# VectorE sums issued behind a pair's eviction, and one more Strassen round in each of the last two chunks

## The chip, the cores and the metric

The kernel runs on one core of one Trainium2 chip. The metric is the device time of one execution in microseconds. "PE" is TensorE, "DVE" VectorE, "ACT" ScalarE, "POOL" GpSimd, "SP" SyncE; "PEld" is TensorE's loading of stationary operands, which runs beside its matmuls.

## The reference

Causal attention with 16 beacon rows ahead of the keys, followed by two matrix products with a leaky ReLU between them:

```python
# B, H, S, Nb, D = 8, 8, 576, 16, 64
k_all = np.concatenate([beacon_k, k], axis=2); v_all = np.concatenate([beacon_v, v], axis=2)
scores = scale * np.matmul(q, k_all.transpose(0, 1, 3, 2))      # causal on the 576 keys
a = softmax(scores)
attn = np.matmul(a, v_all)
x = attn.transpose(0, 2, 1, 3).reshape(B * S, H * D)            # 4608 x 512
h = x @ w_in                                                    # 512 -> 2048
out = np.maximum(0.01 * h, h) @ w_out                           # 2048 -> 512
```

Inputs and output are float32; the kernel computes its products in bfloat16 and sums in float32.

## The kernel before

**Attention.** The 64 heads are taken as 32 pairs. For a pair TensorE writes scores into PSUM (`score` for the first 8 pairs, `stretch` after them, three tiles of 512 columns in a `block`), ScalarE takes their exponentials into a buffer `aT`, GpSimd blanks the triangles above the diagonal (`triangle`, L285), and TensorE multiplies by the values (`value_matmuls`, L355) in two halves of three and two row blocks. `value` then evicts each half on VectorE: a reciprocal of the sums (L384) and a product into `x_nat` (L385). A DMA transpose turns `x_nat` into `xT`. The values of a batch come in five loads that GpSimd issues (L210), and so do queries and keys (L167).

**The two layers.** The 4608 tokens are 9 chunks of 512. `up` computes one block of 128 of the 2048 hidden columns (`moe1`, L438: four matmuls of 512 columns, then an eviction on ScalarE, L446), 16 of them a chunk. `down` computes one of 14 pieces of layer two, which is a Strassen-Winograd scheme of seven products (`moe2`, L514: eight matmuls of 256 columns a piece). That scheme needs sums of the hidden values, the token sums: `token_sums` gives four VectorE operations for each half of the columns, at L789. They wait in a list `due`, and `add_due` issues one ahead of each `up` or `down`; `add_all` issues what a chunk still lacks ahead of its third product.

**The last two chunks** (numbers 7 and 8) come after the attention. There a part of layer one is done in rounds: `in_round` computes four blocks with seven products of four 256-column matmuls each (L667) where four `up`s take sixteen of 512 columns. Its products are combined by five VectorE sums (L710, L721, L722, L724, L725) and leave over ScalarE (`leave`, L684). `last_chunks` reads the order from a string: `R111` is a round with one `down` at each of three places in it, `u` an `up`, `d` a `down`, `t` the token sums of the first half, `x` the sums of the chunk's tokens that the rounds read. Chunk 7 has two rounds and eight `up`s before the change, chunk 8 three and four.

**What sets the order.** Each engine runs its instructions in the order in which they are written. Attention and layers are interleaved by a list of events with places along the pairs. Between two events `fill` issues `up`s and `down`s, and ahead of a `value` event it does so until two (or four, where no `down` can run) stand between the last block of scores and the values. All of them, the score tiles of a block's first tile and the halves of the values share one pool of four PSUM banks (`ps_one`), handed out again in the order in which the program gives them back.

Of the kernel before, what the change touches and what calls it, by code (L numbers as in the profile page):

```python
# [15 lines left out]
def kernel(  # L16
# [11 lines left out]
    nc = tc.nc  # L28

    B, H, S, D = q.shape  # L30
# [7 lines left out]
    NF = DF // 128  # L38
    NCH = NTOK // 512
# [408 lines left out]
    HF, HD, HT = NF // 2, DM // 2, 256  # L448
# [54 lines left out]
    def ND(i):  # L503
        return 2 * len(PRODUCTS)
# [118 lines left out]
    def w_in_sums(n, lo=0, hi=ROUNDS, first=False):  # L623
        cols = slice(lo * 256, hi * 256)
        (b11, b21), (b12, b22) = (
            [w_in_sb[i][:, at : at + 2, cols] for at in (0, 2)] for i in range(2)
        )
        x, y = {5: (b12, b11), 6: (b22, w_t[5][:, :, cols]), 4: (b21, w_t[6][:, :, cols]), 7: (b22, b12)}[n]
        at = 0 if first else len(due)
        due[at:at] = [  # L630
            (TAIL - 1, dict(out=w_t[n][:, j, cols], in0=x[:, j], in1=y[:, j], op=SUB)) for j in range(2)
        ]

    def x_parts(i):
        at = i * 512 % (XR * S)
# [19 lines left out]
    def in_product(i, n, r, bank, first):  # L655
        (a11, a12), (_, a22) = x_parts(i)
        x = {1: a11, 2: a12, 4: a22}.get(n)
        x = x_sums[i][n] if x is None else x
        for f in range(2):
            cols = slice(r * 256 + f, r * 256 + f + 255, 2)  # L660
            for j in range(2):
                if n in w_t:
                    w = w_t[n][:, j, cols]
                else:
                    i0, j0 = {1: (0, 0), 2: (0, 2), 3: (1, 2)}[n]
                    w = w_in_sb[i0][:, j0 + j, cols]
                nc.tensor.matmul(  # L667
                    out=bank[:, f * HT : (f + 1) * HT],
                    lhsT=w,
                    rhs=x[:, j],  # L670
                    start=first and f == 0 and j == 0,
                    stop=j == 1,
                    skip_group_check=True,
                )

    leaves = []

    def leave_all(n=3):
        while leaves and n:
# [11 lines left out]
    def in_round(i, r, downs):  # L691
        if i not in gT:
            gT[i] = gpool.tile([128, NF, 512], BF16, name="gT")
        add = nc.vector.tensor_tensor

        def bank():
            return ps_one.tile([128, 512], FP32, name="acc", tag="one")

        one = bank()
        in_product(i, 1, r, one, True)  # L700
        nc.scalar.copy(out=temps["p1"], in_=one)
        leave_all(1)
# [18 lines left out]
        add(out=temps["u3"], in0=seven, in1=temps["u2"], op=ADD)  # L721
        add(out=temps["c21"], in0=four, in1=temps["u3"], op=ADD)  # L722
        in_product(i, 3, r, five, False)
        add(out=temps["c12"], in0=five, in1=temps["u2"], op=ADD)  # L724
        add(out=temps["c22"], in0=temps["u3"], in1=temps["p5"], op=ADD)  # L725
        leaves.extend(((i, 2 * r, 1, temps["c21"]), (i, HF + 2 * r, 0, temps["c12"]), (i, HF + 2 * r, 1, temps["c22"])))
        for _ in range(downs[2]):
            down()
        done1[0] += 4

    def last_chunks(steps):
        for step in steps.split():
            op, n = step[0], int(step[1:] or 1)
            i = done1[0] // NF
            if op == "d":
                for _ in range(n):
                    down()
            elif op == "u":
                for _ in range(n):
                    leave_all()  # L740
                    up()
            elif op == "R":
                in_round(i, done1[0] % NF // 4, [int(x) for x in step[1:]])
            elif op == "X":
                x_transposes(n, nc.vector.tensor_copy)
            elif op == "w":
                w_in_sums(7, ROUNDS - 1, ROUNDS)
            elif op == "x":
                x = x_in_sums(n)
                if n == TAIL:  # L750
                    for _, op in x[:2]:
                        nc.vector.tensor_tensor(**op)
                    due[2:2] = [x[3], x[2]]
                else:
                    due.extend(x)
            elif op == "a":
                add_due(n)
            elif op == "D":
                later = due[:]
                assert len(later) == 4, len(later)  # L760
                due.clear()
                down()
                down()
                due.extend(later)
            elif op == "t":
                leave_all()
                due.extend((i, op) for op in token_sums(i, 0, SLICE))

    done1, done2, at2, ready, turn, first_down, held = [0], [0], [0, 0], [0], [0], [0], [0]

# [13 lines left out]

    due = []

    def add_due(n=1):
        while due and n:
            nc.vector.tensor_tensor(**due.pop(0)[1])  # L789
            n -= 1  # L790

    def add_all(i):
        while due and due[0][0] == i:
            add_due()

    SLICE = 4
    first_sums = {}

    def up():
        i1, n = divmod(done1[0], NF)  # L800
        assert i1 < ready[0]
        add_late()
        fc = n if i1 == 0 else n // 2 + n % 2 * HF
# [12 lines left out]
        if i1 and n % (2 * SLICE) == 2 * SLICE - 1:  # L816
            due.extend((i1, op) for op in token_sums(i1, n // 2 + 1 - SLICE, n // 2 + 1))

    def down():
        add_late()  # L820
# [130 lines left out]
    with order:  # L951
# [22 lines left out]
        def has_down():  # L974
            return at2[0] < done1[0] // NF
# [79 lines left out]
```

## Time and profile before

| | |
|---|---|
| median of three runs | 323.6 us (323.35 to 325.74) |
| the profiled execution | 323.36 us, of which the span of the trace is 321.7 us |
| TensorE busy | 315.4 us of the span (98%) |
| VectorE, ScalarE, GpSimd busy | 172.8, 207.3, 184.8 us |
| granted TensorE clock | 0.999 |

Times inside the trace are counted from the start of the span. In a timeline a row gives the start, the length from the first start to the last end, the engine, the line, the operation with its operands, and in brackets how long the engine stood idle before it and who released it. In the chain of waits a row gives start, length and what ran. In a grouped view a row ends in the busy time and the mean of one in ns.

### The profile page before, as it was taken

What the parts mean: (1) busy time and instruction counts of PE and PEld (TensorE: products, weight loads), DVE (VectorE), ACT (ScalarE), POOL (GpSimd) and SP (SyncE); (2) the same over time, 40 slices, a digit from 0 to 9 for tenths busy, and PEclk for the clock granted to TensorE, in tenths of its full rate; (3) what the DMA queues carried; (4) which work ended last, traced back from release to release, by engine and by line L of the source; (5) the groups of instructions that cost most, each with busy time, mean ns of one, the idle gap of its engine ahead of it and who ended that gap; (6) DMA issues with size and microseconds to landing.
All of it is one profiled execution on the core that took longest, in us unless ns stands there. A gap on an engine that the chain in (4) does not pass through costs nothing.

```text
span 321.7 us, 8891 instructions
## 1 busy us (share of the span) xinstructions
PE 315.4 (98%) x3578; PEld 225.0 (70%) x3578; DVE 172.8 (54%) x350; ACT 207.3 (64%) x352; POOL 184.8 (57%) x352
## 2 busy tenths in 40 slices
PE   8999999999999999999999999999999999999995
PEld 5584558765677558845888888656865687688784
DVE  3473378635365145434552454435464699577954
ACT  3979974489756786478647864787468446555510
POOL 8896939999999687659875976765221000000000
PEclk9999999999999999999999999999999999999999
DMA  7999999999999999999999999999312101200113
GB/s 133 137 199 200 137 208 134 127 189 195 139 142 177 191 136 152 122 159 117 144 154 181 111 142 117 156 159 122 71 49 87 24 0 35 92 9 7 67 61 131
DMA packets 152474, 39.51 MB, mean 123 GB/s; under 512 B 138816, under 2 KB 150208, under 8 KB 152432
## 3 DMA queue, kind: packets, MB, share of 16 engines
q0 software_dynamic: 97744, 18.54, 85.0%
q1 hardware_dynamic: 54416, 20.33, 37.4%
q8 instruction: 28, 0.46, 0.7%
q14 instruction: 14, 0.11, 0.1%
q10 hardware_dynamic: 272, 0.07, 0.1%
HBM read 37.22 MB, written 9.44 MB: 145 GB/s over the span
## 4 chain that ended last, share of the span: by engine, by line
PE 92%; ACT 5%; DVE 1%; issue 1%; ACTq 0%
PE acc L438 31%; PE acc L514 23%; PE sc L514 11%; PE av L355 9%; PE sc L310 6%; PE acc L667 5%; PE sc L263 2%; PE av L835 2%; ACT aT L329 2%; PE tp L239 2%; ACT gT L446 1%; ACT aT L325 1%; PE tp L401 1%; ACT aT L272 1%; DVE x_nat L385 0%
## 5 line engine op out<-in xcount | busy, mean ns | idle before, releaser
L438 PE MATMUL acc<-xT,w_in_sb 128*128 128x512 bf16 (+1 forms) x560 | 117.6, 355 | 0.4 <-DVE x_nat L385 0.4
L446 ACT ACTIVATE gT<-acc 128x512 bf16<-128x512 f32 x124 | 71.2, 626 | 33.0 <-PE acc L438 32.8
L285 POOL TENSOR_SCALAR_AFFINE_SELECT aT<-aT 128x256 bf16<-128x256 bf16 (+2 forms) x160 | 60.3, 406 | 53.9 <-ACT aT L325 29.6
L438 PEld LDWEIGHTS <-w_in_sb 128*128 128x128 bf16 x560 | 51.8, 98 | 43.4 <-issue 2.3
L514 PEld LDWEIGHTS <-gT 128*128 128x128 bf16 x576 | 54.9, 98 | 9.5 <-issue 2.0
L329 ACT ACTIVATE aT<-sc 128x1024 bf16<-128x1024 f32 (+3 forms) x64 | 51.8, 894 | 0.0
L514 PEld LDWEIGHTS <-gsum 128*128 128x128 bf16 x432 | 40.9, 98 | 7.6 <-issue 0.6
L325 ACT ACTIVATE aT<-sc 128x512 bf16<-128x512 f32 (+3 forms) x64 | 29.0, 521 | 23.0 <-PE sc L310 23.0
L384 DVE RECIPROCAL rec<-av 128x6 f32<-128x6 f32 (+1 forms) x64 | 11.9, 186 | 55.2 <-PE av L355 54.6
L355 PEld LDWEIGHTS <-aT 128*128 128x128 bf16 (+1 forms) x960 | 36.2, 98 | 7.6 <-issue 0.4
L355 PE MATMUL av<-v_aug,aT 128*128 128x65 bf16 (+1 forms) x960 | 38.7, 194 | 0.0
L210 POOL DMA_DIRECT2D v_aug<-in_v_dram x40 | 34.2, 864 | 3.0 <-DMA w_in_sb<-in_moe_w_in_dram 3.0
L514 PE MATMUL acc<-w_out_sb,gT 128*128 128x256 bf16 x288 | 34.6, 273 | 0.4 <-ACT gT L446 0.4
L167 POOL DMA_DIRECT2D k_nat<-in_k_dram x46 | 33.4, 733 | 0.8 <-issue 0.6
L167 POOL DMA_DIRECT2D q_nat<-in_q_dram x46 | 33.4, 731 | 0.1
L385 DVE TENSOR_TENSOR x_nat<-av,rec 128x384 bf16<-128x384 f32 (+1 forms) x64 | 31.4, 491 | 2.2
L272 ACT ACTIVATE aT<-sc 128x1024 bf16<-128x1024 f32 (+3 forms) x32 | 25.8, 872 | 3.2 <-PE sc L263 3.2
L789 DVE TENSOR_TENSOR gsum<-gT 128x1024 bf16<-128x1024 bf16 x18 | 12.4, 689 | 24.3 <-ACT gT L446 24.3
L514 PE MATMUL acc<-w_sum,gsum 128*128 128x256 bf16 x192 | 24.3, 273 | 0.0
L310 PE MATMUL sc<-qT,kT 64*128 64x80 bf16 (+22 forms) x384 | 22.2, 251 | 0.6 <-DVE x_nat L385 0.4
L310 PEld LDWEIGHTS <-kT 64*128 64x128 bf16 x384 | 12.9, 94 | 10.6 <-issue 6.7
L545 ACT COPY p<-acc 128x512 f32<-128x512 f32 x15 | 9.1, 605 | 14.9 <-PE acc L514 14.9
(95 smaller groups left out, 337.3 us busy)
## 6 DMA issues: line engine op xcount, KB each, us to landing
out_dram<-p SPq DMA_DIRECT2D x26, 256.0 KB, 2.9
q_nat<-in_q_dram POOLq DMA_DIRECT2D x46, 72.0 KB, 4.9
k_nat<-in_k_dram POOLq DMA_DIRECT2D x46, 72.0 KB, 5.3
v_aug<-in_v_dram POOLq DMA_DIRECT2D x24, 128.0 KB, 6.1
w_in_sb<-in_moe_w_in_dram POOLq DMA_DIRECT2D x2, 1024.0 KB, 11.0
w_out_sb<-in_moe_w_out_dram POOLq DMA_DIRECT2D x2, 1024.0 KB, 11.4
out_dram<-u SPq DMA_DIRECT2D x8, 256.0 KB, 3.5
gsum<-in_q_dram POOLq DMA_DIRECT2D x9, 144.0 KB, 7.5
```

The costliest lines, as they stand in the source:

```text
L167: nc.gpsimd.dma_start(out=t[:, :, par], in_=(q, k)[which][b, 2 * hp + par].rearrange("(t p) d -> p t d", p=NR),)
L210: nc.gpsimd.dma_start(out=dst[lo : ROWS[c], c, :, 0:D], in_=v[b, :, OFF[c] : OFF[c] + n].rearrange("h p d -> p h d"),)
L272: nc.scalar.activation(out=aT[:, :, c0 : c0 + w], in_=sc[:, :, 0:w], func=AF.Exp, scale=0.125)
L285: nc.gpsimd.affine_select(out=view, in_=view, compare_op=ALU.is_ge, fill=0.0, base=128 - n if lo == 0 else 0, channel_multiplier=-1, patte ...
L310: nc.tensor.matmul(out=(sc[par] if apart else sc[:, par])[:, at : at + b - a], lhsT=kT[ps_, c * 128 : (c + 1) * 128], rhs=qT[ps_, q0 : q0 ...
L325: nc.scalar.activation(out=probs[g][:, par, lo:hi], in_=sc[par][:, at : at + hi - lo], func=AF.Exp, scale=0.125)
L329: nc.scalar.activation(out=probs[g][:, :, lo:hi], in_=sc[:, :, at : at + hi - lo], func=AF.Exp, scale=0.125)
L355: nc.tensor.matmul(out=avv[:, n, 0 : D + 1], lhsT=aT[0 : ROWS[c], par, a0 : a0 + 128], rhs=va[0 : ROWS[c], c, 2 * hp + par, :], start=(c = ...
L385: nc.vector.tensor_tensor(out=x_nat[:, t0:t1].rearrange("p t e d -> p (t e) d"), in0=avv[:, :, 0:D], in1=rec[:, n0:n1, None].to_broadcast( ...
L438: nc.tensor.matmul(out=acc[:, lo:hi], lhsT=w_in_cols(fc, j), rhs=xT[:, j, x0 : x0 + hi - lo], start=(j == 0), stop=(j == NJ - 1), skip_gro ...
L446: nc.scalar.activation(out=gT[i][:, fc, :], in_=acc, func=AF.Prelu, alpha=0.01)
L514: nc.tensor.matmul(out=acc[:, lo : lo + HD], lhsT=left(i, n, fc, tile), rhs=right(n, fc), start=(lo == 0 and fc == 0), stop=(fc == HF - 1) ...
```

## The change

**Behind the eviction.** While an event `value` is prepared, `add_due` only counts what it would have issued; the operations are issued right behind that half's eviction. `add_all` now picks a chunk's operations out of the list wherever they stand, and a round first issues the sums of its chunk's tokens that are still owed.

**One more round.** Chunk 7 has three rounds and four `up`s, chunk 8 four rounds and no `up`. The weight sums of the fourth round (`w_in_last`, eight operations of 128x256) are made on GpSimd into the value buffer of the last but one batch. The sum `c22` of each round (L725 before) moves from VectorE to GpSimd. Two weight sums that were made between chunk 7 and chunk 8 are made in chunk 6.

```diff
+    flat_v = v_bufs[(B - 2) % 2].rearrange("p c h d -> p (c h d)")
+    w_last = {
+        n: flat_v[:, i * 512 : (i + 1) * 512].rearrange("p (j f) -> p j f", j=2) for i, n in enumerate((5, 6, 4, 7))
+    }
...
+    def w_in_last(n, eng):
+        cols = slice(ROUNDS * 256, (ROUNDS + 1) * 256)
...
+        for j in range(2):
+            eng.tensor_tensor(out=w_last[n][:, j], in0=x[:, j], in1=y[:, j], op=SUB)
...
     def in_product(i, n, r, bank, first):
...
+            if any(op["out"] is x for _, op in due):
+                add_all(i, [x_sums[i][m] for m in (5, 6, 3, 7)])
...
-                    w = w_t[n][:, j, cols]
+                    w = w_t[n][:, j, cols] if r < ROUNDS else w_last[n][:, j, f : f + 255 : 2]
...
-        add(out=temps["c22"], in0=temps["u3"], in1=temps["p5"], op=ADD)
+        nc.gpsimd.tensor_tensor(out=temps["c22"], in0=temps["u3"], in1=temps["p5"], op=ADD)
...
+    owed = [None]
+
     def add_due(n=1):
+        if owed[0] is not None:
+            owed[0] += n
+            return
         while due and n:
             nc.vector.tensor_tensor(**due.pop(0)[1])
             n -= 1
...
+        if (i1, n) == (TAIL - 1, 4 * ROUNDS + 1):
+            w_in_sums(7, ROUNDS - 1, ROUNDS, first=True)
+            add_due(2)
...
             elif what is value:
+                owed[0] = owed[0] or 0
                 while done1[0] + done2[0] < since + (2 if has_down() else 4) and fill(True):
                     pass
             what(*args)
+            if what is value:
+                n, owed[0] = owed[0], None
+                add_due(n)
...
-        last_chunks("D X31 x7 d a1 R111 x8 R111 t u d u d u d u u d u d u u w")
-        last_chunks("R111 R111 R111 t u d u d u d u d d d14")
+        for n in (5, 6, 4, 7):
+            w_in_last(n, nc.gpsimd)
+        last_chunks("D X31 x7 d a1 R110 R111 x8 u R311 d t u u u")
+        last_chunks("R100 R112 t d R200 R111 d d d t3 d14")
```

VectorE's order in the middle of the attention, at the first pair whose values meet the token sums of chunk 1 (`gsum` is a token sum, `gT` the hidden values and one token sum in place, `av` a half of the values in PSUM). Before:

```order
L789 TENSOR_TENSOR gsum_1608<-gT 128x1024
L789 TENSOR_TENSOR gsum_1609<-gsum_1608,gT 128x1024
L384 RECIPROCAL rec<-av 128x6
L385 TENSOR_TENSOR x_nat<-av,rec 128x384
L384 RECIPROCAL rec<-av 128x4
L385 TENSOR_TENSOR x_nat<-av,rec 128x256
L789 TENSOR_TENSOR gT<-gT 128x4x256
L789 TENSOR_TENSOR gsum_1610<-gT,gsum_1609 128x1024
```

And at the same place after the change:

```order
L384 RECIPROCAL rec<-av 128x6
L385 TENSOR_TENSOR x_nat<-av,rec 128x384
L813 TENSOR_TENSOR gsum_1608<-gT 128x1024
L813 TENSOR_TENSOR gsum_1609<-gsum_1608,gT 128x1024
L813 TENSOR_TENSOR gT<-gT 128x4x256
L813 TENSOR_TENSOR gsum_1610<-gT,gsum_1609 128x1024
L384 RECIPROCAL rec<-av 128x4
L385 TENSOR_TENSOR x_nat<-av,rec 128x256
```

The first half's eviction has moved ahead of two sums; all four sums now stand between the halves, and the second half's eviction behind four of them instead of two.

VectorE's order two pairs later, at the other half of chunk 1's token sums. Before:

```order
L789 TENSOR_TENSOR gsum_1608<-gT 128x1024
L384 RECIPROCAL rec<-av 128x6
L385 TENSOR_TENSOR x_nat<-av,rec 128x384
L384 RECIPROCAL rec<-av 128x4
L385 TENSOR_TENSOR x_nat<-av,rec 128x256
L789 TENSOR_TENSOR gsum_1609<-gsum_1608,gT 128x1024
L789 TENSOR_TENSOR gT<-gT 128x4x256
L789 TENSOR_TENSOR gsum_1610<-gT,gsum_1609 128x1024
```

And after the change:

```order
L384 RECIPROCAL rec<-av 128x6
L385 TENSOR_TENSOR x_nat<-av,rec 128x384
L813 TENSOR_TENSOR gsum_1608<-gT 128x1024
L813 TENSOR_TENSOR gsum_1609<-gsum_1608,gT 128x1024
L384 RECIPROCAL rec<-av 128x4
L385 TENSOR_TENSOR x_nat<-av,rec 128x256
L813 TENSOR_TENSOR gT<-gT 128x4x256
L813 TENSOR_TENSOR gsum_1610<-gT,gsum_1609 128x1024
```

The first half's eviction has moved ahead of one sum, and the second half's stands behind two instead of one.

GpSimd's order at the end of the program, from the triangles of the last pair on (`aT_93` is that pair's buffer, later the place of `c22`; `v_aug_88` the value buffer that takes the fourth round's weight sums). Before:

```order
L285 AFFINE_SELECT aT_93<-aT_93 128x2x112
L285 AFFINE_SELECT aT_93<-aT_93 128x2x128 x3
L285 AFFINE_SELECT aT_93<-aT_93 80x2x80
L1050 UNCONDITIONAL_BRANCH
L1050 ISA
```

And after the change:

```order
L285 AFFINE_SELECT aT_93<-aT_93 80x2x80
L645 TENSOR_TENSOR v_aug_88<-w_in_sb_83,w_in_sb_82 128x256 x2
L645 TENSOR_TENSOR v_aug_88<-w_in_sb_83,v_aug_88 128x256 x2
L645 TENSOR_TENSOR v_aug_88<-w_in_sb_82,v_aug_88 128x256 x2
L645 TENSOR_TENSOR v_aug_88<-w_in_sb_83 128x256 x2
L742 TENSOR_TENSOR aT_93<-kT 128x512 x7
```

GpSimd, which ended with the last triangles, now makes the eight weight sums behind them, and then one `c22` for each of seven rounds.

More of the change, by code (lines that the diff above doesn't have):

```diff
@@ L632, in w_in_sums @@
         ]
+    def w_in_last(n, eng):
+        cols = slice(ROUNDS * 256, (ROUNDS + 1) * 256)
+        (b11, b21), (b12, b22) = (
+            [w_in_sb[i][:, at : at + 2, cols] for at in (0, 2)] for i in range(2)
+        )
+        x, y = {5: (b12, b11), 6: (b22, w_last[5]), 4: (b21, w_last[6]), 7: (b22, b12)}[n]
+        for j in range(2):
+            eng.tensor_tensor(out=w_last[n][:, j], in0=x[:, j], in1=y[:, j], op=SUB)
     def x_parts(i):
@@ L674, in in_product @@
                 )
-    leaves = []
+    ROUNDS_OF = (3, 4)
+    leaves, plain, rounds = [], {}, {}
     def leave_all(n=3):
@@ L734, in last_chunks @@
             i = done1[0] // NF
+            if op == "t" and n == 3 and done1[0] % NF == 0:
+                i -= 1
             if op == "d":
@@ L766, in last_chunks @@
                 leave_all()
-                due.extend((i, op) for op in token_sums(i, 0, SLICE))
+                assert rounds[i] >= n
+                due.extend((i, op) for op in token_sums(i, n // 3 * SLICE, (n // 3 + 1) * SLICE))
     done1, done2, at2, ready, turn, first_down, held = [0], [0], [0, 0], [0], [0], [0], [0]
@@ L790, in add_due, with add_all @@
             n -= 1
-    def add_all(i):
-        while due and due[0][0] == i:
-            add_due()
+    def add_all(i, only=None):
+        mine = [x for x in due if x[0] == i and (only is None or any(x[1]["out"] is t for t in only))]
+        due[:] = [x for x in due if all(x is not m for m in mine)]
+        for _, op in mine:
+            nc.vector.tensor_tensor(**op)
     SLICE = 4
@@ L802, in up @@
         add_late()
-        fc = n if i1 == 0 else n // 2 + n % 2 * HF
+        if i1 < TAIL:
+            fc = n if i1 == 0 else n // 2 + n % 2 * HF
+        else:
+            plain[i1] = m = plain.get(i1, -1) + 1
+            fc = 2 * ROUNDS_OF[i1 - TAIL] + m // 2 + m % 2 * HF
         moe1(i1, fc)
@@ L815, in up @@
                 due.extend((0, first_sums[m][k]) for k in (1, 2, 3) for m in (11, 15))
-        if i1 and n % (2 * SLICE) == 2 * SLICE - 1:
+        if i1 and n % (2 * SLICE) == 2 * SLICE - 1 and (i1 < TAIL or n == NF - 1):
             due.extend((i1, op) for op in token_sums(i1, n // 2 + 1 - SLICE, n // 2 + 1))
     def down():
+        assert at2[0] < done1[0] // NF and all(x[0] != at2[0] for x in leaves)
         add_late()
@@ L1020 @@
             what(*args)
+            if what is value:
+                n, owed[0] = owed[0], None
+                add_due(n)
         assert at2 == [TAIL - 1, ND(TAIL - 1) - LEFT] and done1[0] == TAIL * NF, (at2, done1)
         apart_from_values[0] = True
-        last_chunks("D X31 x7 d a1 R111 x8 R111 t u d u d u d u u d u d u u w")
-        last_chunks("R111 R111 R111 t u d u d u d u d d d14")
+        for n in (5, 6, 4, 7):
+            w_in_last(n, nc.gpsimd)
+        last_chunks("D X31 x7 d a1 R110 R111 x8 u R311 d t u u u")
+        last_chunks("R100 R112 t d R200 R111 d d d t3 d14")
+        assert at2[0] == NCH and not (due or late or leaves)
 _INS = ['q', 'k', 'v', 'beacon_k', 'beacon_v', 'moe_w_in', 'moe_w_out']
```

8 lines of the change are left out of this document (4 added, 4 removed).

## Prediction

> **What bounds the kernel now.** I read the first part of the page, then what TensorE waited for (waiter, line, releaser: us in total, times, longest).
>
> ```profile
> PE 315.4 (98%) x3578; PEld 225.0 (70%) x3578; DVE 172.8 (54%) x350; ACT 207.3 (64%) x352; POOL 184.8 (57%) x352
> PE av L835 <- DVE blank L917: 1.1, 1, 1.1
> PE acc L438 <- DVE x_nat L385: 0.4, 1, 0.4
> PE acc L514 <- ACT gT L446: 0.4, 2, 0.2
> PE sc L310 <- DVE x_nat L385: 0.4, 1, 0.4
> ```
>
> TensorE is busy for all but 6.3 of the span's 321.7 us, and waits by name for 2.3 us. Only the two waits for `x_nat`, the eviction of the values, are of the kind that the change touches. The rest is TensorE's own work, so a gain has to come from fewer matmuls or from these two places. The ends of matmuls are modelled, so a wait is worth more than the idle time shown; I take it from starts.
>
> **The last two chunks.** Their part of the chain of waits (start, length, what):
>
> ```profile
> 273.94 0.87 PE sc L514 x8
> 274.82 1.73 PE acc L438 x8
> ...
> 293.56 1.31 PE acc L667 x12
> ```
>
> No other engine stands in it: TensorE follows itself. A round is 28 matmuls of 1.31 / 12 = 0.109 us, 3.06 us. The four `up`s that it replaces are two such rows of eight, 2 x 1.73 = 3.46 us. One round saves 0.40 us, two save **0.80 us**, as long as rounds and their sums keep feeding TensorE. The `down`s only change places.
>
> Whether they do hangs on VectorE and GpSimd. The sums of a round, with their evictions on ScalarE:
>
> ```profile
> 268.33 0.69 DVE L721 TENSOR_TENSOR kT<-acc,kT 128x512 f32<-128x512 f32 x1 [0.18 <-PE acc L667]
> 269.13 0.69 DVE L722 TENSOR_TENSOR aT<-acc,kT 128x512 f32<-128x512 f32 x1
> 269.74 0.68 DVE L724 TENSOR_TENSOR kT<-acc,kT 128x512 f32<-128x512 f32 x1
> 270.33 0.68 DVE L725 TENSOR_TENSOR aT<-kT 128x512 f32<-128x512 f32 x1
> 271.05 0.63 ACT L684 ACTIVATE gT<-aT 128x512 bf16<-128x512 f32 x1
> 281.00:304.00 23.00, 23.00 (x197) 19.03 (x196) 17.90 (x30) 13.71 (x25) 0.00 (x0) 1.00 0.10 33
> ```
>
> The last row is a stretch of 23 us: PE, PEld, DVE, ACT and POOL busy. VectorE has 5.1 us to spare there. The two added rounds bring 2 x 5 x 0.69 us of sums, and moving `c22` (L725) takes 7 x 0.68 away: 2.1 us more in all of the 49 us of both chunks. No VectorE trouble in the sum.
>
> On GpSimd no two-input sum stands in the trace. Its nearest rows, whole run:
>
> ```profile
> L285 POOL TENSOR_SCALAR_AFFINE_SELECT aT<-aT 128x256 bf16<-128x256 bf16 x96 | 39.9, 430 | 51.4 <-ACT aT L325 29.2 <-ACT aT L329 15.2 <-ACT aT L272 3.8
> L184 POOL CAST bk<-bk_raw 128x384 bf16<-128x384 f32 x1 | 0.5, 499 | 0.0
> ```
>
> From below: 512 columns at the cast's 1.30 ns each, 0.67 us. From above: the triangle's 1.68 ns, doubled for the second input, 1.72 us. I take twice the cast, 1.33 us, the row in the same type. **What hides it:** `c22` needs only `u3` (L721, done at 269.02) and p5. On VectorE it queued behind `c21` and `c12` and ended at 271.01; on GpSimd it may start at 269.05 and ends by 270.4. It is late only above **2.0 us**, so both bounds cost nothing. By the Trainium skill's GPSIMD Engine Reference, section 3.1, a float32 sum of 2048 columns takes 4497 ns; a quarter of that is an estimate of 1.1 us, and the sum would be the same by it.
>
> The eight weight sums on GpSimd are half as wide: 0.33 to 0.86 us each by the same rows, 2.7 to 6.9 us behind its last triangles at 245.4. Their reader is the fourth round of chunk 8, over 40 us later. Cover enough. The two weight sums that move into chunk 6 take 0.28 us each and go into idle time of VectorE there.
>
> **First place in the attention.** VectorE and TensorE, timelines:
>
> ```profile
> 74.95 1.09 PE L355 MATMUL av<-v_aug,aT 128*128 128x65 bf16 x30
> 75.26 0.70 DVE L789 TENSOR_TENSOR gsum<-gT 128x1024 bf16<-128x1024 bf16 x1 [3.75 <-ACT gT L446]
> 75.98 1.10 PE L310 MATMUL sc<-qT,kT 64*128 64x96 bf16 x16
> 76.00 0.77 DVE L789 TENSOR_TENSOR gsum<-gsum,gT 128x1024 bf16<-128x1024 bf16 x1
> 76.69 0.18 DVE L384 RECIPROCAL rec<-av 128x6 f32<-128x6 f32 x1
> 76.91 0.56 DVE L385 TENSOR_TENSOR x_nat<-av,rec 128x384 bf16<-128x384 f32 x1
> 77.52 3.63 PE L438 MATMUL acc<-xT,w_in_sb 128*128 128x512 bf16 x16 [0.44 <-DVE x_nat L385]
> 80.99 1.08 PE L355 MATMUL av<-v_aug,aT 128*128 128x65 bf16 x30
> 81.56 0.20 DVE L384 RECIPROCAL rec<-av 128x6 f32<-128x6 f32 x1 [2.17 <-PE av L355]
> ```
>
> The first half's eviction stood behind two sums until 76.69, and the next `up` needs its bank. Undisturbed, the reciprocal comes 0.57 us after the values start (80.99 to 81.56), so now at 75.52, and the bank is free at 76.3. Scores hand over about 0.07 us ahead of their modelled end, so the `up` can start at 77.0 instead of 77.52: 0.52 us. What is late next: the second half, behind four sums. They take about 2.8 us (the pitches here are 0.74 and 0.69, then 0.60 and 0.78), so it is out at 79.7. In the changed program its bank goes to the fourth `up`, due at 77.0 + 3 x 0.865 = 79.6 (an `up` is 1.73 / 2). That gives back 0.1; **0.4 us** stay.
>
> **Second place.**
>
> ```profile
> 87.17 1.04 PE L514 MATMUL acc<-w_sum,gT 128*128 128x256 bf16 x8
> 87.73 0.56 DVE L385 TENSOR_TENSOR x_nat<-av,rec 128x384 bf16<-128x384 f32 x1
> 88.35 0.18 PE L310 MATMUL sc<-qT,kT 64*128 64x16 bf16 x1
> 88.42 0.42 DVE L385 TENSOR_TENSOR x_nat<-av,rec 128x256 bf16<-128x256 f32 x1
> 88.90 0.85 PE L310 MATMUL sc<-qT,kT 64*128 64x16 bf16 x15 [0.37 <-DVE x_nat L385]
> ```
>
> Eight matmuls from 87.17 are over at 88.04; the scores start at 88.35, and their second bank is free only at 88.84. With the first half out by 86.8 and the second bank no longer this pair's, they run on from 88.04: **0.86 us**. TensorE is then 1.26 us ahead.
>
> **What is late next.** A lead is kept only if nothing on another clock is waited for. From 56 to 98 us GpSimd is such a clock (columns as above), and one load that it issues has hardly any slack:
>
> ```profile
> 56.00:98.00 42.00, 40.98 (x451) 28.13 (x450) 20.30 (x39) 29.75 (x55) 41.99 (x76) 1.00 1.91 158
> 91.76 0.73 POOL L210 DMA_DIRECT2D v_aug<-in_v_dram  x1
> v_aug<-in_v_dram POOLq DMA_DIRECT2D x1, 80.0 KB, 7.2
> 98.85 0.72 PE L355 MATMUL av<-v_aug,aT 128*128 128x65 bf16 x18
> 99.02 0.56 PE av L355 x18
> ```
>
> GpSimd works 41.99 of 42 us, so it gains nothing when TensorE runs ahead. The load of a batch's last 80 rows is issued at 91.76 and lands 7.2 us later (the DMA view of 91 to 93 us), at 98.96. Its first reader is the 13th of the 18 matmuls that start at 98.85, at 0.031 us each (0.56 / 18): 99.22. The slack is 0.26, less 0.05 for the release. So I expect a **new wait of about 1.05 us** there, and **0.2 us** of the 1.26 left. After 100 us GpSimd has idle time again and follows; the 0.2 stays. The two waits for ScalarE's `gT` (0.4 us by name) are not touched.
>
> Elsewhere the moved sums push an eviction back. The tightest such place:
>
> ```profile
> 147.75 0.56 DVE L385 TENSOR_TENSOR x_nat<-av,rec 128x384 bf16<-128x384 f32 x1
> ...
> 148.82 0.69 DVE L789 TENSOR_TENSOR gsum<-gT,gsum 128x1024 bf16<-128x1024 bf16 x1
> 149.12 3.56 PE acc L438 x16
> ```
>
> The two sums behind this eviction, of which the second ends at 148.82 + 0.69 = 149.51, now stand ahead of it, so it is out at 149.5 at the latest instead of 148.31. In the changed program its bank goes to the second `up` of the chain's row, at 149.12 + 0.865 = 149.98. It costs nothing while 0.5 us of cover hold; without it, 0.1 to 0.6 us once or twice in the run.
>
> **Sum**, against the profiled execution's 323.36 us: 323.36 - 0.80 - 0.20 = 322.36. The median of the runs lies 0.24 above that execution and the lowest run at it; I keep **322.4 us**.
>
> **Rivals.**
> 1. *The lead stays whole*: the load lands earlier too, or TensorE meets nothing else. For it: nothing names this load as waited for today. Against: GpSimd's 41.99 of 42. 323.36 - 0.80 - 1.26 = 321.3.
> 2. *The attention gives nothing, or takes a little*: transfers that now start earlier (stores, transposes) hold the 80-row load up by as much as the 0.2. 322.6, with a half microsecond of delay 323.0.
> 3. *Slower: GpSimd's `c22` is the bound of a round.* It decides above 2.0 us. At 3.0 us each round gets `c22` 1.0 us late, and its eviction on ScalarE and the copies queued behind that one with it. Three of the seven rounds are followed by the next with one or two `down`s between; there some 0.65 of the 1.0 us reach TensorE, since ScalarE is busy 13.71 of 23 us and takes up the rest. 322.4 + 3 x 0.65 = 324.4, slower than before. Against it: the bounds 0.67 to 1.72.
> 4. *Nothing of the change does what it says*: sums are only moved, and rounds replace `up`s one for one in time. 323.4. The 0.109 us per matmul speak against it.
> 5. *VectorE and GpSimd block each other.* Beside triangles a sum of VectorE is longer:
>
> ```profile
> 237.00 1.01 POOL L285 TENSOR_SCALAR_AFFINE_SELECT aT<-aT 128x256 bf16<-128x256 bf16 x3 [0.30 <-PE av L355]
> 237.72 0.83 DVE L542 TENSOR_TENSOR u<-u,p 128x512 f32<-128x512 f32 x1
> ```
>
> 0.83 against 0.69 us, 0.14 more. If a sum instead waits out a whole `c22`, seven times 1.33 - 0.69 = 0.64 at most, and half of it reaches TensorE, 322.4 + 2.2 = 324.6. This is what the Trainium skill's SBUF — State Buffer, section "Who interferes with whom", would make of it: a VectorE instruction with two SBUF inputs and a GpSimd instruction that reads SBUF exclude each other for the whole instruction. By that rule the sum at 237.72 would have ended 0.29 late, at the triangles' end plus 0.69; it ended 0.14 late, so the trace shows less than the rule. For `c21` and `c12`, which run right beside `c22`, one input is in PSUM, and the page names no block.
>
> **How the numbers follow.** Chances: forecast 0.48, rival 1 0.17, rival 2 0.16, rival 3 0.08, rival 4 0.05, rival 5 0.06. The range 321.1 to 323.8 holds the forecast and rivals 1, 2 and 4, and leaves rivals 3 and 5 above it. One per cent is 3.2 us, about what a measurement of this kernel can tell from no change; both gains whole, with ScalarE's waits on top, stay under it. Faster by over 1%: 0.02; slower: 0.03, from a larger price in rivals 3 and 5; the rest within.
>
> **What would show it.** In the changed profile: no wait of TensorE for `x_nat` at 77 and 88 us; a wait of L355 near 98 us, released by the `v_aug` DMA, of about 1 us (none: rival 1); GpSimd's 128x512 sum below 2.0 us; 196 matmuls on the line of the rounds (7 x 28, 140 now) and 32 fewer than the 560 on L438, with TensorE not idle between 255 and 300 us. What would make me wrong: a wait of the rounds for `c22` or for VectorE (upward), or the load of the 80 rows landing with TensorE's lead (downward).

## The result: slower by 1.3%

The changed kernel takes 328.6 us (median of six executions, 327.45 to 329.31), the kernel before 324.2 us beside it (323.35 to 325.74). The ratio is 1.0132, with a 95% interval of 1.0109 to 1.0155. The forecast of 322.4 us, with a range up to 323.8, was wrong, and the sign of the change with it. The profiled execution takes 327.45 us (span 325.7) against 323.36 (321.7).

The page's first part and, of its second, the row of granted clocks (40 equal slices, in tenths), after:

```profile
PE 314.0 (96%) x3577; PEld 227.1 (70%) x3602; DVE 179.2 (55%) x353; ACT 209.2 (64%) x356; POOL 199.2 (61%) x367
...
PEclk9999999999999999999999999999999799999999
```

and what TensorE waited for (waiter, line, releaser: us in total, times, longest), its two longest:

```profile
PE av L355 <- DVE x_nat L385: 2.0, 1, 2.0
PE sc L310 <- DMA kT<-k_nat: 1.9, 1, 1.9
```

TensorE is busy for 1.4 us less (some records of matmuls are missing in a trace, so the rounds' gain is better read below), and it has two waits of 2 us that before did not have. The 7 among the clocks is new as well. The order of the matmuls is the same in both programs until 255 us, so each matmul of after can be held against the same one of before. The shift between their starts, worked out from the two traces:

```
start before   shift after    what lies between
 69.3 us       +0.18 us       first loads, different in each execution
 84.1          -0.30          the old wait at 77.5 us is gone: 0.48
 88.9          -1.05          the old waits at 88.4 and 88.9 are gone: 0.75
 89.2          +1.05          new wait for kT: 2.10
249.2          +1.05          nothing in 160 us
249.4          +3.21          new wait for x_nat: 2.16
252.3          +4.87          low clock: 1.66
317.8 (end)    +4.11          two more rounds: -0.76
```

In some executions the first 20 us take longer, by 3.8 to 6.4 us in the profiles of e4, e9 and e10; ratios leave the longest executions out, as do the medians given for e5 and e12, and shifts are read between two places of one trace.

**The wait for kT.** The timeline of VectorE and then of SP's queue (start, length, what), after:

```profile
75.93 0.56 DVE L385 TENSOR_TENSOR x_nat<-av,rec 128x384 bf16<-128x384 f32 x1
76.40 0.68 DVE L813 TENSOR_TENSOR gsum<-gT 128x1024 bf16<-128x1024 bf16 x1
...
78.33 0.89 DVE L813 TENSOR_TENSOR gsum<-gT,gsum 128x1024 bf16<-128x1024 bf16 x1
79.15 0.17 DVE L384 RECIPROCAL rec<-av 128x4 f32<-128x4 f32 x1
79.35 0.42 DVE L385 TENSOR_TENSOR x_nat<-av,rec 128x256 bf16<-128x256 f32 x1
79.80 1.19 SPq L413 DMA_TRANSPOSE xT<-x_nat  x1
81.04 1.23 SPq L421 DMA_TRANSPOSE xT<-x_nat  x1
82.44 1.64 SPq L175 DMA_TRANSPOSE qT<-q_nat  x1
84.19 1.21 SPq L175 DMA_TRANSPOSE kT<-k_nat  x1
```

its chain of waits there (start, length, what):

```profile
84.19 6.00 DMA kT<-k_nat
...
90.24 0.56 PE sc L310 x6
```

and, before, the second half on VectorE and the same transposes in SP's queue:

```profile
77.59 0.42 DVE L385 TENSOR_TENSOR x_nat<-av,rec 128x256 bf16<-128x256 f32 x1
...
78.04 1.19 SPq L413 DMA_TRANSPOSE xT<-x_nat  x1
79.28 1.22 SPq L421 DMA_TRANSPOSE xT<-x_nat  x1
80.68 1.21 SPq L175 DMA_TRANSPOSE qT<-q_nat  x1
82.00 1.21 SPq L175 DMA_TRANSPOSE kT<-k_nat  x1
```

The first half leaves earlier, as meant. The second half stands behind four sums and is out at 79.77 instead of 78.01. SP sends the transposes of `x_nat` 0.03 us behind that, in both kernels, and behind them in its queue stand the q and k transposes of a later pair. So kT is issued 2.19 us later, takes 6.00 us, and lands at 90.19; the first score that needs it starts at 90.24 and could have started at 88.1.

**The wait for x_nat and the clock.** The timeline of VectorE, GpSimd and TensorE near 250 us, after:

```profile
247.40 4.46 DVE L813 TENSOR_TENSOR aT<-w_in_sb,aT 128x768 bf16<-128x768 bf16 x1
251.78 0.18 DVE L384 RECIPROCAL rec<-av 128x6 f32<-128x6 f32 x1
252.00 0.56 DVE L385 TENSOR_TENSOR x_nat<-av,rec 128x384 bf16<-128x384 f32 x1
246.39 1.29 POOL L645 TENSOR_TENSOR v_aug<-w_in_sb,w_in_sb 128x256 bf16<-128x256 bf16 x2
247.65 2.54 POOL L645 TENSOR_TENSOR v_aug<-w_in_sb,v_aug 128x256 bf16<-128x256 bf16 x4
250.16 1.28 POOL L645 TENSOR_TENSOR v_aug<-w_in_sb 128x256 bf16<-128x256 bf16 x2
252.62 0.73 PE L355 MATMUL av<-v_aug,aT 128*128 128x65 bf16 x18 [1.99 <-DVE x_nat L385]
```

and that stretch by windows (length; busy time of PE, PEld, DVE, ACT, POOL; then the granted clock):

```profile
250.00:252.00 2.00, 0.62 (x3) 0.10 (x1) 1.97 (x2) 0.99 (x2) 1.45 (x3) 1.00 0.12 25
252.00:254.00 2.00, 1.38 (x22) 0.90 (x23) 2.00 (x5) 0.00 (x0) 0.00 (x0) 0.92 0.00 0
254.00:256.00 2.00, 1.78 (x5) 0.70 (x5) 1.97 (x5) 0.60 (x1) 0.00 (x0) 0.50 0.00 0
256.00:258.00 2.00, 2.00 (x18) 1.20 (x17) 1.02 (x5) 0.60 (x2) 0.00 (x0) 0.72 0.28 57
```

The same sum of VectorE before:

```profile
246.35 0.55 DVE L789 TENSOR_TENSOR aT<-w_in_sb,aT 128x768 bf16<-128x768 bf16 x1
```

It took 0.55 us and is now shown as 4.46 us long. It ends at 251.86, 0.42 us behind the last of GpSimd's eight weight sums (251.44). It asks for a semaphore of GpSimd's, whose triangles were over at 246.42, and it reads nothing that the weight sums write; that the program does not make it wait for the row is shown by e9 below. The eviction behind it is late, the bank is not free, and TensorE stands for 2.16 us. From 253.7 to 257.1 us the granted clock is then 0.5 (windows of half a microsecond).

### The profile page after: what moved, and what is told of

Read it like the earlier page. It is cut to its first block, busy times and chain, and to the rows that moved or that the text cites. A ratio compares the mean times of both kernels' runs of the same rounds, so it can differ in the third digit from the quotient of the medians.

```text
span 325.7 us, 8955 instructions
## 1 busy us (share of the span) xinstructions
PE 314.0 (96%) x3577; PEld 227.1 (70%) x3602; DVE 179.2 (55%) x353; ACT 209.2 (64%) x356; POOL 199.2 (61%) x367
## 4 chain that ended last, share of the span: by engine, by line
PE 88%; ACT 4%; DMA 3%; issue 2%; DVE 1%; SPq 0%; ACTq 0%; POOLq 0%
PE acc L438 27%; PE acc L514 22%; PE sc L514 11%; PE av L355 9%; PE acc L683 7%; PE sc L310 6%; PE sc L263 2%; DMA kT<-k_nat 2%; PE tp L239 2%; ACT aT L329 2%; DMA gsum<-in_q_dram 1%; ACT gT L446 1%; ACT aT L325 1%; PE av L869 1%; PE tp L401 1%
## 5 line engine op out<-in xcount | busy, mean ns | idle before, releaser
L438 PE MATMUL acc<-xT,w_in_sb 128*128 128x512 bf16 (+1 forms) x503 | 109.1, 355 | 1.6 <-issue 0.4
L446 ACT ACTIVATE gT<-acc 128x512 bf16<-128x512 f32 x116 | 66.2, 626 | 31.1 <-PE acc L438 31.1
L438 PEld LDWEIGHTS <-w_in_sb 128*128 128x128 bf16 x528 | 48.9, 98 | 41.5 <-issue 3.8
L742 POOL TENSOR_TENSOR aT<-kT 128x512 f32<-128x512 f32 x7 | 8.9, 1276 | 48.1 <-DVE kT L738 31.2
```

What stands on the lines that cost most here:

```text
L438: nc.tensor.matmul(out=acc[:, lo:hi], lhsT=w_in_cols(fc, j), rhs=xT[:, j, x0 : x0 + hi - lo], start=(j == 0), stop=(j == NJ - 1), skip_gro ...
L446: nc.scalar.activation(out=gT[i][:, fc, :], in_=acc, func=AF.Prelu, alpha=0.01)
```

## The experiments

### The weight sums on GpSimd (e1, e2, e3, e9)

e1 moves the eight sums behind chunk 7:

```diff
-        for n in (5, 6, 4, 7):
-            w_in_last(n, nc.gpsimd)
         last_chunks("D X31 x7 d a1 R110 R111 x8 u R311 d t u u u")
+        for n in (5, 6, 4, 7):
+            w_in_last(n, nc.gpsimd)
         last_chunks("R100 R112 t d R200 R111 d d d t3 d14")
```

> The changed kernel, but the eight weight sums of the fourth round stand on GpSimd behind chunk 7's steps instead of behind the last triangles. Theory A (GpSimd's sums hold VectorE's two-input sum of 128x768 up for 4.46 us at 247.4 us of the changed profile, its eviction comes late, TensorE waits 2.17 us at 250.2 and its clock then falls to 0.5, another 1.66 us): no such wait and no clock below 1 there, 327.45 - 2.17 - 1.66 = 323.6 us for the profiled run, about 1.2% under the changed kernel. VectorE's two-input sums will be long at the new place, near 290 us, where TensorE has other work. Rival B (the order on VectorE is at fault: one more sum ahead of that eviction): the wait stays, 327.5 us. Rival C (the clock falls there whatever is waited for): the wait goes, the low clock stays, 325.3 us.

Measured: ratio to before 1.0046 (1.0024 to 1.0068), profile 325.22 us. No wait and no low clock at 250 us: theory A; B and C fall. The profile lies above the 323.6 because the first loads took 0.75 us more than before's and because of a wait in chunk 8's first round. What stands side by side there, in its timeline, and TensorE's wait:

```profile
282.01 0.99 DVE L813 TENSOR_TENSOR gsum<-gT 128x1024 bf16<-128x1024 bf16 x1
283.04 1.04 DVE L813 TENSOR_TENSOR gsum<-gsum,gT 128x1024 bf16<-128x1024 bf16 x1
281.79 3.90 POOL L645 TENSOR_TENSOR v_aug<-w_in_sb,v_aug 128x256 bf16<-128x256 bf16 x4
```

```profile
PE acc L683 <- DVE kT L727: 0.7, 1, 0.7
```

Here the two engines take turns: VectorE's sums of 0.69 us last 1.0 to 1.2, GpSimd's of 0.64 last 0.97. That is dear too, but VectorE is not shut out.

e2 is the kernel before with nothing but these eight sums, in the place where the change puts them (`w_in_last` as in the change):

```diff
...
+        for n in (5, 6, 4, 7):
+            w_in_last(n, nc.gpsimd)
         last_chunks("D X31 x7 d a1 R111 x8 R111 t u d u d u d u u d u d u u w")
```

> The kernel before, and nothing else than the eight 128x256 weight sums on GpSimd behind the last triangles (nobody reads them). Theory A: one 128x768 sum of VectorE near 246.4 us grows from 0.55 us to over 4 us, TensorE waits about 2 us and loses up to 1.7 us more to the clock: 325.4 to 327.2 us. Rival B (order on VectorE): as the kernel before, 323.4 us.

Measured: 1.0086 (1.0053 to 1.0120), profile 326.35 us. The sum of VectorE is 4.47 us long, TensorE's shift grows by 2.18 us at 249.4 us, and the order on VectorE is that of before. So these sums alone are enough. In this profile the clock stays at 1.00; in two of the eight executions it is 0.995, and those take 328.7 and 329.1 us.

e3 makes them twice:

```diff
-        for n in (5, 6, 4, 7):
+        for n in (5, 6, 4, 7) * 2:
             w_in_last(n, nc.gpsimd)
```

> The changed kernel with the eight weight sums on GpSimd made twice, 16 in a row. Theory A with VectorE held until GpSimd's whole row is over: the row is 5.1 us longer, VectorE's sum lasts 9.6 us instead of 4.46, TensorE waits 7.3 us instead of 2.17: 332.6 us, plus what the clock takes. Theory A with only one GpSimd instruction waited for at a time: the sum stays near 4.5 us, 327.5 us. Rival B: 327.5 us.

VectorE and the end of GpSimd's row in its timeline, and TensorE's longest wait:

```profile
249.54 9.47 DVE L813 TENSOR_TENSOR aT<-w_in_sb,aT 128x768 bf16<-128x768 bf16 x1
257.31 1.28 POOL L645 TENSOR_TENSOR v_aug<-w_in_sb 128x256 bf16<-128x256 bf16 x2
```

```profile
PE av L355 <- DVE x_nat L385: 7.0, 1, 7.0
```

The sum is 9.47 us long, against 9.6 expected, and ends 0.4 us behind GpSimd's sixteenth. VectorE is held for the whole row, not for one instruction. The profile takes 335.61 us, 3 us over the 332.6, which held 1.66 us of low clock: by the shift it is 1.6 us behind the wait for kT and 2.6 behind this one.

e9 leaves the row in its place and puts an instruction that reads nothing between:

```diff
             eng.tensor_tensor(out=w_last[n][:, j], in0=x[:, j], in1=y[:, j], op=SUB)
+            if j == 0:
+                nc.gpsimd.memset(flat_v[:, 2048:2560], 0.0)
...
             w_in_last(n, nc.gpsimd)
+            nc.gpsimd.memset(flat_v[:, 2048:2560], 0.0)
```

> The changed kernel with a memset of 128x512 (it writes and reads nothing) on GpSimd behind each of the eight weight sums. Theory A1 (what holds VectorE is that GpSimd's next reading instruction follows at once): VectorE's 128x768 sum gets in at the first memset, lasts 1.2 us or less instead of 4.46, and the wait of 2.17 us at 250 us shrinks below 0.3 us; profile 323.6 to 324 us. Theory A2 (GpSimd holds VectorE off for its whole row, whatever stands in it): the sum is as long as the row, longer than 4.46 us by the memsets, and the wait grows.

The beginning of GpSimd's row in its timeline, and VectorE's sum:

```profile
252.49 0.66 POOL L645 TENSOR_TENSOR v_aug<-w_in_sb,w_in_sb 128x256 bf16<-128x256 bf16 x1
253.10 0.52 POOL L647 MEMSET v_aug<- 128x512 bf16 x1
253.58 0.66 POOL L645 TENSOR_TENSOR v_aug<-w_in_sb,w_in_sb 128x256 bf16<-128x256 bf16 x1
254.19 0.52 POOL L1065 MEMSET v_aug<- 128x512 bf16 x1
253.49 1.17 DVE L815 TENSOR_TENSOR aT<-w_in_sb,aT 128x768 bf16<-128x768 bf16 x1
```

The sum lasts 1.17 us (this profile runs 6 us later than before's from its first 20 us on). It came 0.09 us ahead of GpSimd's second sum and ended 0.42 us behind it, beside the memset. TensorE has no wait there. Ratio 1.0016 (0.9993 to 1.0040); the two lowest executions take 323.5 and 323.9 us, at a clock of 1.0, the next two 325.4 and 325.5 at 0.994. A1 holds: GpSimd's row is 3.8 us longer than in the changed kernel, and this sum loses 0.6 us instead of 3.9. Later VectorE rows beside the spaced row are still 0.5 to 0.6 us longer than in the kernel before; nobody waits for them.

By the Trainium skill's SBUF — State Buffer, section "Who interferes with whom", a VectorE instruction with two SBUF inputs and a GpSimd instruction that reads SBUF exclude each other for the whole instruction. The trace agrees on the pair (1.17 us beside e9's memsets), and differs on the length: the loser waited out six further instructions at 247.4 us, and the rest of a row of sixteen in e3. In e1 a sum of VectorE and one of GpSimd took 1.0 to 1.1 us together, less than the 1.33 of one behind the other. Why turns were taken in e1 and not here stays open. Who came first does not settle it: in e1 VectorE's sum at 282.01 also came in the middle of GpSimd's row. Every long hold here is of one and the same sum, which reads `w_in_sb` as GpSimd's sums do, while those that took turns in e1 read other tiles; whether that matters no run tests.

### The queue of SP (e4, e5, e6, e7)

e4 takes the owed operations out of the changed kernel and leaves the rest:

```diff
             elif what is value:
-                owed[0] = owed[0] or 0
...
-            if what is value:
-                n, owed[0] = owed[0], None
-                add_due(n)
```

> The changed kernel with the token and weight sums issued where they were before (ahead of the values), the rounds and everything else as changed. Theory D (behind the second half's late eviction the transposes of x_nat, q and k stand in SP's queue, so that kT lands 2.1 us late at 90.2 us and takes the 1.23 us of lead and 0.87 more): no wait for kT; the two old waits for x_nat are back; 327.45 - 0.87 = 326.6 us, with the loss at 250 us unchanged. Rival E (kT is late for another reason, the loads or the state of the DMA queues): 327.5 us with that wait still there.

Measured: 1.0090 (1.0058 to 1.0122); the two lowest executions take 326.1 and 326.6 us at a clock of 1.0, the next two 328.1 at 0.993. No wait for kT, the two old waits back (0.5 and 0.4 us by name), the wait at 250 us as it was. So the wait for kT comes with the owed operations.

e5 is e1 with one pair's transposes moved ahead in SP's queue; the order on the other engines is the same:

```diff
-                events.append((at + 0.38, 5, x_turn, (g,)))
+                events.append((at + (1.1 if g == FIRST else 0.38), 5, x_turn, (g,)))
```

> The kernel with late weight sums (e1), and on SP's queue alone two pairs of rows changed places: the q and k transposes of one pair (kT issued at 84.2 us of the changed profile) stand ahead of the two x_nat transposes that waited there for the late second half (79.8 us). VectorE, GpSimd, ScalarE and TensorE keep their order. Theory D (SP's queue): no wait for kT at 90 us; of the 2.0 us that it cost either all comes back (e1's profile 325.2 becomes 323.2 us) or, if the load of the last 80 rows of the values at 98 us clips the lead as was forecast, 1.2 us with a wait of about 1 us for v_aug (324.0 us). Rival E (the k load, the DMA queues or the number of transfers make kT late): the wait stays, 325.2 us.

SP's queue in its timeline, and the value matmuls that need the last 80 rows:

```profile
76.79 1.20 SPq L175 DMA_TRANSPOSE qT<-q_nat  x1
78.92 1.20 SPq L175 DMA_TRANSPOSE kT<-k_nat  x1
80.22 1.21 SPq L413 DMA_TRANSPOSE xT<-x_nat  x1
98.12 0.35 PE L355 MATMUL av<-v_aug,aT 80*128 80x65 bf16 x6 [0.23 <-DMA v_aug<-in_v_dram]
```

kT goes out at 78.92, the wait at 90 us is gone, VectorE being as late as ever. The lead is 1.23 us at 88.9 us. At 98.12 the load of the last 80 rows takes 0.39 of it (from starts), and 0.84 stays to the end of the attention. The profile takes 322.33 us, the median is 324.0, ratio to before 0.9994 (0.9960 to 1.0028), against 1.0046 for e1. Theory D holds, E falls.

e6 issues the owed sums behind the second half alone, on top of e1:

```diff
-            if what is value:
+            if what is value and args[1] == 1:
                 n, owed[0] = owed[0], None
```

> The kernel with late weight sums (e1), but what is owed while values are prepared is issued behind the eviction of the second half instead of behind each half, so that no eviction stands behind a sum. Theory D: x_nat's transposes go out near 76.5 us, kT is early, no wait at 77, 88 or 90 us; the lead of 1.2 us either stays (322.9 to 323.2 us) or is clipped at 98 us by v_aug (324.0 us). Rival E: the wait for kT stays, 325.2 us.

The same matmuls in its timeline, and TensorE's longest waits:

```profile
99.82 0.35 PE L355 MATMUL av<-v_aug,aT 80*128 80x65 bf16 x6 [1.08 <-DMA v_aug<-in_v_dram]
```

```profile
PE acc L514 <- DVE gsum L813: 2.5, 2, 1.8
```

No wait for kT, and here the load of the 80 rows costs 1.25 us from starts, where the forecast had put 1.05. But it is no repair: 1.0059 (1.0028 to 1.0089). The sums now come later than `down`s that need them, 1.9 us at 160 us and 0.9 at 193 (from starts). The expectation did not have this.

e7 is the first part of the change alone, on the kernel before (`owed`, `add_due` and `add_all` as in the change):

```diff
...
+                owed[0] = owed[0] or 0
...
+            if what is value:
+                n, owed[0] = owed[0], None
+                add_due(n)
```

> The kernel before with the first part of the change alone: sums issued behind each half's eviction; old rounds, no weight sums on GpSimd. Theory D: lead 1.2 us at 88.9 us, then a wait of 2 us for kT: 0.9 us slower than before, 324.2 us against 323.4. The forecast's theory (1.26 us of lead, clipped to 0.2 by v_aug): 323.2 us. No wait at 250 us and no low clock in either.

Measured: 1.0043 (1.0011 to 1.0076). The wait for kT is there with 2.1 us, and TensorE's shift goes from +1.84 us at 60 to 75 us (first loads) to +0.62 at 88.9, then to +2.90, and stays. The four lowest of twelve executions take 324.4 us, close to the 324.2 of theory D; five with a clock of 0.993 to 0.995 take 325.8 to 326.7. The forecast's theory falls: the part that was to bring 0.2 us costs about 1, and in some executions 1.4 to 2.3 more.

### The rounds (e8), TensorE's clock (e10), another place for the sums (e11)

e8 is e1 without the owed operations, so rounds, `c22` on GpSimd, late weight sums and the two sums in chunk 6 are what is left of the change:

```diff
-                owed[0] = owed[0] or 0
...
-            if what is value:
-                n, owed[0] = owed[0], None
-                add_due(n)
```

> The kernel before with the two added rounds and c22 on GpSimd, its sums issued ahead of the values as before, and the weight sums of the fourth round late (as in e1). The forecast's term: 0.80 us less than before, against which stand up to 0.85 us of the wait that e1 showed in chunk 8's first round, since the late weight sums run beside VectorE's: 322.6 to 323.4 us. A rival (the rounds are slower than their matmuls, for c22 or VectorE): above 323.4 us, with waits of L683 in every round.

Measured: 0.9981 (0.9956 to 1.0006), profile 322.97 us, of which 0.45 us are luck in the first loads. Over the last two chunks TensorE's shift rises by 0.09 us: the rounds' 0.76, and against it the wait of L683 (0.7 us by name, 0.85 from starts). No other round waits. Where the sums are not late (the changed kernel, e4, e9, e12) the shift falls by 0.75 to 0.76 us there, so the rival falls.

e10 keeps TensorE busy while it would wait at 250 us (`filler` issues matmuls of zeros):

```diff
...
+            if what is value and args == (NG - 2, 1):
+                filler(9)
             what(*args)
```

> The changed kernel with nine matmuls of 512 zero columns (9 x 0.216 = 1.94 us; their result is read by nobody) on TensorE ahead of the values that wait 2.17 us at 250 us. VectorE is as late as before, so nothing is gained by the matmuls themselves. Theory F (idle time of TensorE of about 2 us is what lowers the granted clock): idle there falls to 0.2 us, no clock of 0.5 at 254 to 257 us, 327.45 - 1.66 = 325.8 us, and executions that show a clock of 0.988 in the changed kernel show at most 0.994, those with 0.994 up to 1.0. Rival G (the clock falls for the load that follows, or at that time of the program): 327.5 us, the low clock stays.

VectorE's held sum and the nine matmuls in its timeline, then the two windows in which the clock had been low:

```profile
250.87 4.47 DVE L813 TENSOR_TENSOR aT<-w_in_sb,aT 128x768 bf16<-128x768 bf16 x1
253.93 2.10 PE L880 MATMUL sc<-blank 128*128 128x512 bf16 x9
```

```profile
254.00:256.00 2.00, 2.00 (x10) 0.71 (x8) 1.97 (x4) 0.60 (x1) 0.92 (x2) 1.00 0.08 14
256.00:258.00 2.00, 1.89 (x25) 1.20 (x26) 1.97 (x7) 0.28 (x1) 0.00 (x0) 1.00 0.03 8
```

VectorE is as late as before, the shift grows by the same 2.18 us, and the clock stays at 1.00. The lowest executions take 325.6 and 326.0 us at 1.0 and 327.3 at 0.995 (the profiled one 329.3, at 0.984, its low clock lies in the first 20 us); the changed kernel has 327.4 to 328.2 at 0.994 and 329.0 to 329.3 at 0.988. The ratio, 1.0093 (1.0059 to 1.0127), lies under the changed kernel's 1.0132, though the intervals overlap. The trace alone would not show theory F, since e2's clock stayed at 1.00 with the wait unfilled. What speaks for F is the count: of the changed kernel's six executions none has a clock of 1.0, here four of six have. That supports F and leaves room for chance.

e11 is e5 with the eight sums on VectorE, in the list of due operations of chunk 7 (the step `W` calls `w_in_last`):

```diff
...
-            eng.tensor_tensor(out=w_last[n][:, j], in0=x[:, j], in1=y[:, j], op=SUB)
+            due.append((TAIL + 1, dict(out=w_last[n][:, j], in0=x[:, j], in1=y[:, j], op=SUB)))
...
-        last_chunks("D X31 x7 d a1 R110 R111 x8 u R311 d t u u u")
+        last_chunks("D X31 x7 d a1 R110 R111 W x8 u R311 d t u u u")
```

> The kernel of e5 (the two SP transposes ahead) with the eight weight sums on VectorE, one by one between chunk 7's pieces, instead of on GpSimd: nothing of GpSimd but c22 then stands beside VectorE's sums. Theory A: e5's last wait (0.85 us of TensorE at 284 us in chunk 8's first round) goes: 322.33 - 0.85 = 321.5 us for the profile, 0.6% under the kernel before. Rival (VectorE's 8 x 0.28 us more are what the rounds then wait for): 322.3 us or more, with waits of the rounds for VectorE.

TensorE's longest wait:

```profile
PE sc L514 <- DVE gsum L824: 3.0, 1, 3.0
```

A miss: 1.0123 (1.0105 to 1.0141). The list hands out one operation per piece, so eight more push chunk 7's token sums to the point where a `down` needs all of them at once, and TensorE waits 3.0 us; the clock is 0.994 or 0.995 in all four executions. By the trace it is the order on VectorE that made the wait, more than its time.

### Both repairs (e12)

e12 is the changed kernel with e9's memsets and e5's line:

```diff
+            if j == 0:
+                nc.gpsimd.memset(flat_v[:, 2048:2560], 0.0)
...
-                events.append((at + 0.38, 5, x_turn, (g,)))
+                events.append((at + (1.1 if g == FIRST else 0.38), 5, x_turn, (g,)))
...
             w_in_last(n, nc.gpsimd)
+            nc.gpsimd.memset(flat_v[:, 2048:2560], 0.0)
```

> The changed kernel with both repairs: the memsets between GpSimd's weight sums (e9) and the q and k transposes of the one pair ahead on SP's queue (e5). No wait for kT at 90 us, none for x_nat at 250 us, no low clock behind them, no wait in chunk 8's first round. From e9's lowest executions (323.5 us) the 0.95 us that kT's wait cost beyond the lead, and 0.84 us of lead that e5 kept: 321.7 us, 0.6% under the kernel before. If the lead is clipped further than in e5, up to 322.6 us. If the two mechanisms are not the causes, 323.5 us or more.

TensorE's longest waits:

```profile
PE av L355 <- DMA v_aug<-in_v_dram: 1.4, 1, 1.4
PE av L871 <- DVE blank L953: 1.1, 1, 1.1
PE tp L239 <- DMA gsum<-in_q_dram: 0.8, 1, 0.8
```

The median is 322.4 us against 324.4 for the kernel before beside it, the ratio 0.9935 (0.9906 to 0.9964); the lowest is 321.35. Both new waits are gone, the clock is 1.0 in every execution, and the wait for the 80 rows that the forecast named is the longest of all. In this profile (323.20 us) it takes 1.58 us, more than the lead of 1.22, where e5 lost 0.39: the load was issued at 91.21 and took 8.6 us here, at 91.74 and 6.3 us in e5. That, and 0.26 us in the first loads, is nearly all of the distance to the 321.7 I expected.

## Why the prediction was wrong

- **First and second place: right.** 0.48 and 0.75 us gained, against 0.52 and 0.86. The lead at 88.9 us is 1.23, forecast 1.26.
- **"What is late next: the second half" is the step that failed first.** Its time was right (out at 79.77, forecast 79.7), and only one reader of it was followed: the bank, where it cost nothing to speak of. The other reader is SP's queue, which carries kT for another pair. The step was costed at 0.1 us; the wait that came of it was 2.10, which took the lead of 1.23 and 0.87 more (e4, e5, e7).
- **"The eight weight sums ... Cover enough" failed second.** I asked who reads them and when. I did not ask what VectorE has to run beside them. Rival 5 had the mechanism, and I tied it to `c22`, whose neighbours `c21` and `c12` have one input in PSUM; they lasted 0.69 us beside it, as forecast. Its price, at most 0.64 us a time, was mis-sized too: this row was waited out whole, 3.9 us (e2, e3; e9 breaks it).
- **The clock was not in the sum.** A wait of 2 us was followed by a low clock in some executions, which cost 1.66 us in this profile and as much behind the wait for kT in e3. That the wait is its cause is supported by e10. No rival had it.
- **The new wait at 98 us: right in kind.** It does not show in the changed kernel, since the lead was gone by then. It shows wherever kT is on time: 0.39 (e5), 1.25 (e6) and 1.58 us (e12) from starts, forecast 1.05. The forecast took the load at the 7.2 us of one profile; it took 6.3 to 8.6.
- **The rounds: right.** 0.76 us against 0.80, with 196 weight loads on their line and 528 on L438, and no wait of TensorE there. `c22` on GpSimd, in the page's groups (busy time and mean ns, idle time before):

```profile
L742 POOL TENSOR_TENSOR aT<-kT 128x512 f32<-128x512 f32 x7 | 8.9, 1276 | 48.1 <-DVE kT L738 31.2 <-issue 16.9
```

  1.28 us, forecast 1.33, and nobody waits for it. The 5.1 us that VectorE had to spare were no cover in themselves, though: e11 put 2.3 us more of sums on VectorE in these chunks and TensorE waited 3.0.
- **The tight place at 149 us** cost nothing: the shift is +1.05 from 90 to 249 us.

Together 323.36 + 0.18 (first loads) - 1.23 + 2.10 + 2.16 + 1.66 - 0.76 = 327.47, the profile's 327.45. Of these the forecast has the 1.23 and the 0.76. With both missed waits repaired (e12), the median is the 322.4 us of the forecast, but that is in part luck: in e12's profile the attention loses 0.36 us (a lead of 1.22, a wait of 1.58) where the forecast gained 0.20, and by the ratio e12 gains 0.65% (0.36 to 0.94), the forecast 0.37.

## What to carry to other kernels

When an instruction is pushed back, follow each of its readers and then what stands behind that reader in its queue: a DMA queue that several pairs share carries the delay to data that has nothing to do with it. A free engine is no place for work whose operands keep another engine out: look at what the neighbour runs at that time, and break the row. And where TensorE is the bound, an interruption of 2 us has to be priced with the low clock that may follow it.

## What the runs showed of the hardware

- A row of GpSimd two-input sums held a two-input SBUF sum of VectorE until the row ended (4.46 us for eight, 9.47 for sixteen; always the one sum at 247 us). A memset of 0.52 us between them let it in. At another place (e1) the two took turns. VectorE's evictions, with one input in PSUM, were not held (0.42 us at 247.06 us beside the row of the changed kernel, 0.42 and 0.56 in e9).
- Waits of TensorE of about 2 us were followed by a granted clock of 0.5, in the changed kernel's profile from 1.1 to 4.5 us after its return, in some executions and not in others. By the mean clock it fell in all six of the changed kernel, which has two such waits, in two of the eight of e2 and two of the six of e4, which have one, and in all four of e11, whose wait is 3.0 us. In e6, whose waits are 1.8 us and less, it stayed at 0.998 or over in all twelve. One execution of e5 (0.993) lies low although its profile has no such wait; where its clock fell is not on record. By the Trainium skill's TensorE: Matmul & The Clock Gate, part 1, the clock halves after an idle window of about 3.4 us that runs on its own count. The halving and the dependence on luck agree with these runs; the length does not, 2.16 us were enough.
- The same load of 80 KB took 6.3 us from issue to landing in e5, 7.2 in the kernel before and in e6, and 8.6 in e12.
